# A DMA-bound `x + alpha * fx`: one fifth of x copied from HBM to HBM, and the scaled fx added to it by an accumulating transfer

## The chip, the cores and the metric

The kernel runs on one core of a Trainium2 chip; the other cores are idle. The metric is the device time of one execution in microseconds (us). All times below are medians of executions in the undisturbed ("fast") state, except for the three runs of a single look, whose state is unknown and which are read for their packets and not for a few per cent of time. The span in a profile is about 1.7 us shorter than the time of the same execution.

## The reference

```
B, S, D = 512, 32, 640            # all bfloat16
x, fx: [B, S, D];  alpha: [1]
def reference(x, fx, alpha):
    return x + alpha * fx
```

x, fx and the output have 20.97 MB each. Both inputs must be read once and the output written once: 62.92 MB.

## The kernel before

The tensors are seen as 128 rows (one for each SBUF partition) of 81,920 elements and cut into five chunks of 128 x 16384, which are 4 MiB each. One queue (that of the sync engine, SP) carries every load and store; VectorE computes each chunk with one instruction.

```
xv  = x.flatten_outer_dims().rearrange("(p n) d -> p (n d)", p=P)     # fxv, ov alike
xs = ...tile_pool(name="xs", bufs=4)      # x tiles, 32 KiB a partition
fs = ...tile_pool(name="fs", bufs=2)      # fx tiles
...
def load_x(k):  ... nc.sync.dma_start(out=xt[k][:], in_=xv[:, bass.ts(k, CHUNK)])
def load_f(k):  ... nc.sync.dma_start(out=ft[k][:], in_=fxv[:, bass.ts(k, CHUNK)])
def compute(k, parts=1): ... nc.vector.scalar_tensor_tensor(   # x = f * a + x
        out=xt[k][:, s], in0=ft[k][:, s], scalar=a_f[:], in1=xt[k][:, s],
        op0=ALU.mult, op1=ALU.add)
def store(k, ...): ... nc.sync.dma_start(out=ov[...], in_=xt[k][...])

load_x(0); load_f(0); load_x(1); load_f(1); load_x(2)
compute(0); load_f(2); store(0); load_x(3)
compute(1); load_f(3); store(1); load_x(4)
compute(2); load_f(4); store(2)
compute(3); store(3)
compute(4, 2); store(4, 0, 2); store(4, 1, 2)      # one statement a line in the source
```

Of the kernel before, what the change touches and what calls it, by code (L numbers as in the profile page):

```python
# [1 line left out]

# [4 lines left out]

ACT = mybir.ActivationFunctionType
ALU = mybir.AluOpType
F32 = mybir.dt.float32  # L10
BF16 = mybir.dt.bfloat16

CHUNK = 16384


def alpha_to_lanes(nc, consts, psum, alpha, eng):

    P = nc.NUM_PARTITIONS
    a_1 = consts.tile([1, 1], alpha.dtype, name="a_1")
    eng.dma_start(out=a_1[:], in_=alpha[None, :])  # L20
    ones = consts.tile([1, P], alpha.dtype, name="ones")
    nc.vector.memset(ones[:], 1.0)  # L22
    a_ps = psum.tile([P, 1], F32, name="a_ps")
    nc.tensor.matmul(a_ps[:], ones[:], a_1[:], start=True, stop=True)  # L24
    a_f = consts.tile([P, 1], F32, name="a_f")
    nc.vector.tensor_copy(out=a_f[:], in_=a_ps[:])  # L26
    return a_f


@with_exitstack  # L30
def kernel(
    ctx: ExitStack,
    tc: tile.TileContext,
    x: bass.AP,
    fx: bass.AP,
    alpha: bass.AP,
    out: bass.AP,
):
    nc = tc.nc
    P = nc.NUM_PARTITIONS  # L40
    xv = x.flatten_outer_dims().rearrange("(p n) d -> p (n d)", p=P)
    fxv = fx.flatten_outer_dims().rearrange("(p n) d -> p (n d)", p=P)
    ov = out.flatten_outer_dims().rearrange("(p n) d -> p (n d)", p=P)
    F = xv.shape[1]
    K = F // CHUNK
    assert K * CHUNK == F and K == 5

    consts = ctx.enter_context(tc.tile_pool(name="consts", bufs=1))
    psum = ctx.enter_context(tc.tile_pool(name="psum", bufs=1, space=bass.MemoryType.PSUM))
    xs = ctx.enter_context(tc.tile_pool(name="xs", bufs=4))  # L50
    fs = ctx.enter_context(tc.tile_pool(name="fs", bufs=2))
    ctx.enter_context(tc.manual_schedule())

    a_f = alpha_to_lanes(nc, consts, psum, alpha, nc.scalar)
    xt, ft = {}, {}

    def load_x(k):
        xt[k] = xs.tile([P, CHUNK], x.dtype, tag="x", name="x_t")
        nc.sync.dma_start(out=xt[k][:], in_=xv[:, bass.ts(k, CHUNK)])  # L59

    def load_f(k):
        ft[k] = fs.tile([P, CHUNK], fx.dtype, tag="f", name="f_t")
        nc.sync.dma_start(out=ft[k][:], in_=fxv[:, bass.ts(k, CHUNK)])

    def compute(k, parts=1):
        n = CHUNK // parts
        for j in range(parts):
            s = bass.ts(j, n)
            nc.vector.scalar_tensor_tensor(  # L69
                out=xt[k][:, s],  # L70
                in0=ft[k][:, s],
                scalar=a_f[:],
                in1=xt[k][:, s],
                op0=ALU.mult,
                op1=ALU.add,
            )

    def store(k, j=0, parts=1):
        n = CHUNK // parts
        nc.sync.dma_start(  # L80
            out=ov[:, k * CHUNK + j * n : k * CHUNK + (j + 1) * n],
            in_=xt[k][:, bass.ts(j, n)],
        )

    load_x(0)
    load_f(0)
    load_x(1)
    load_f(1)
    load_x(2)
    compute(0)  # L90
    load_f(2)
    store(0)
    load_x(3)
    compute(1)
    load_f(3)
    store(1)
    load_x(4)
    compute(2)
    load_f(4)
    store(2)  # L100
    compute(3)
    store(3)
    compute(4, 2)
    store(4, 0, 2)
    store(4, 1, 2)


# [1 line left out]
_INS = ['x', 'fx', 'alpha']  # L109
_OUTS = [((512, 32, 640), 'bfloat16')]  # L110


# [23 lines left out]
```

## Time and profile before

| | before |
|---|---|
| time | 152.34 us (152.24 to 152.45, 2 runs) |
| span in the profile | 150.6 us |
| moved by DMA | 62.92 MB, 418 GB/s |
| SP queue's packets, share of the 16 DMA engines' time | 98.0% |
| VectorE busy | 86.9 us (58%) |

These lines are from the page of the kernel before. First come the busy time of the engines, the DMA row of the 40 equal slices of the span (9 means that the 16 DMA engines were busy for 90% or more), then the queues (packets, MB, share of the time of 16 engines), the HBM traffic, the shares of the chain of waits, the costliest group and the DMA issues (out<-in, number, KB each, median us from issue to landing).

```profile
span 150.6 us, 85 instructions
...
PE 0.2 (0%) x1; PEld 0.1 (0%) x1; DVE 86.9 (58%) x8; POOL 0.2 (0%) x4
...
DMA  6999999999999999799999999999999999999994
...
q1 hardware_dynamic: 2304, 62.92, 98.0%
...
HBM read 41.94 MB, written 20.97 MB: 418 GB/s over the span
...
DMA 56%; DVE 29%; DVEq 6%; issue 0%; SPq 0%
...
L69 DVE SCALAR_TENSOR_TENSOR x_t<-f_t,a_f,x_t 128x16384 bf16<-128x16384 bf16 (+1 forms) x6 | 86.6, 14439 | 49.5 <-DMA f_t<-in_fx_dram 49.5
...
f_t<-in_fx_dram SPq DMA_DIRECT2D x5, 4096.0 KB, 32.1
out_dram<-x_t SPq DMA_DIRECT2D x4, 4096.0 KB, 36.5
```

The DMA row is full and the one queue's packets take 98.0% of the engines' time, so the DMA engines are the limit. VectorE waits 49.5 us for fx, which costs nothing by itself: the transfers that it waits for stand in a full queue. And there are 15 transfers of 4 MiB ("units"): 5 + 5 loads and 5 stores (the last one in halves).

The trace also has a record for each packet. Here they are 32,768 B (one row of a chunk), in the kernel before 1.213 us each in the median, for loads and stores alike: 32768 B / 1.213 us = 27.0 GB/s an engine. All data packets together took 147.5 us of all 16 engines (the sum of their durations over 16), so one unit costs 147.5 / 15 = 9.83 us, and the span has 3.1 us more than the packets fill, for the most part at its start and end (the 6 and the 4 of the DMA row).

### The profile page before, as it was taken

The numbers are of one execution on the slowest core, as the hardware profiler recorded it, in microseconds if no ns is written. First come the engines' busy times: TensorE is split into PE (matmuls) and PEld (weight loads), VectorE is DVE, ScalarE is ACT, GpSimd is POOL, SyncE is SP. The second block draws the span as 40 slices with busy tenths as digits, with TensorE's granted clock in tenths as the row PEclk, the third lists the DMA queues.
The fourth block names the chain that finished last, engine by engine and source line by source line (L and its number), as shares of the span: only waits on it lengthen the run. The fifth ranks groups of instructions, "written<-read, shape, count | busy, mean of one in ns | idle before, by whom it ended". The sixth has DMA issues, their size and how long they took to land.

```text
span 150.6 us, 85 instructions
## 1 busy us (share of the span) xinstructions
PE 0.2 (0%) x1; PEld 0.1 (0%) x1; DVE 86.9 (58%) x8; POOL 0.2 (0%) x4
## 2 busy tenths in 40 slices
PE   0000000000000000000000000000000000000000
PEld 0000000000000000000000000000000000000000
DVE  0000009999679998499991006999900089997000
POOL 0000000000000000000000000000000000000000
DMA  6999999999999999799999999999999999999994
GB/s 200 444 453 435 418 418 418 418 444 453 444 453 435 418 418 418 339 444 470 418 418 418 418 418 435 435 435 453 426 435 444 418 418 435 435 435 405 426 444 205
DMA packets 2306, 62.92 MB, mean 418 GB/s; under 512 B 258, under 2 KB 258, under 8 KB 258
## 3 DMA queue, kind: packets, MB, share of 16 engines
q1 hardware_dynamic: 2304, 62.92, 98.0%
q10 hardware_dynamic: 2, 0.00, 0.0%
HBM read 41.94 MB, written 20.97 MB: 418 GB/s over the span
## 4 chain that ended last, share of the span: by engine, by line
DMA 56%; DVE 29%; DVEq 6%; issue 0%; SPq 0%
DMA f_t<-in_fx_dram 56%; DVE x_t L69 29%; DVEq L131 6%; SPq L59 0%; DVEq L69 0%
## 5 line engine op out<-in xcount | busy, mean ns | idle before, releaser
L69 DVE SCALAR_TENSOR_TENSOR x_t<-f_t,a_f,x_t 128x16384 bf16<-128x16384 bf16 (+1 forms) x6 | 86.6, 14439 | 49.5 <-DMA f_t<-in_fx_dram 49.5
L26 DVE COPY a_f<-a_ps 128x1 f32<-128x1 f32 x1 | 0.2, 159 | 1.1 <-PE a_ps L24 1.1
L22 DVE MEMSET ones<- 1x128 bf16 x1 | 0.2, 165 | 0.8 <-PEq L120 0.8
L24 PE MATMUL a_ps<-a,ones 1*128 1x1 bf16 x1 | 0.2, 159 | 1.9 <-DMA a<-in_alpha_dram 1.9
L120 POOL MEMSET const-bfloat16-1.0<- 128x1 bf16 x1 | 0.1, 102 | 0.0
L120 POOL MEMSET const-uint8-127<- 128x1 uint8 x1 | 0.1, 102 | 0.0
L24 PEld LDWEIGHTS <-ones 1*128 1x128 bf16 x1 | 0.1, 100 | 1.0 <-DVE ones L22 1.0
L120 POOL MEMSET const-float32-0.0<- 128x1 f32 x1 | 0.1, 99 | 0.2 <-issue 0.2
L120 POOL MEMSET const-float32-1.0<- 128x1 f32 x1 | 0.1, 99 | 0.0
## 6 DMA issues: line engine op xcount, KB each, us to landing
x_t<-in_x_dram SPq DMA_DIRECT2D x5, 4096.0 KB, 34.8
f_t<-in_fx_dram SPq DMA_DIRECT2D x5, 4096.0 KB, 32.1
out_dram<-x_t SPq DMA_DIRECT2D x4, 4096.0 KB, 36.5
out_dram<-x_t SPq DMA_DIRECT2D x2, 2048.0 KB, 15.2
a<-in_alpha_dram ACTq DMA_DIRECT2D x1, 0.0 KB
```

Of the source, the lines that this page charges most:

```text
L22: nc.vector.memset(ones[:], 1.0)
L24: nc.tensor.matmul(a_ps[:], ones[:], a_1[:], start=True, stop=True)
L26: nc.vector.tensor_copy(out=a_f[:], in_=a_ps[:])
L69: nc.vector.scalar_tensor_tensor(out=xt[k][:, s], in0=ft[k][:, s], scalar=a_f[:], in1=xt[k][:, s], op0=ALU.mult, op1=ALU.add,)
L120: nc = _bacc.Bacc("TRN2", target_bir_lowering=False, num_devices=1)
L131: with _tile.TileContext(nc) as tc:
```

## The change

The intent is to take one x chunk off the way through SBUF and VectorE: chunk 4 of x is copied from HBM straight to the output, and the scaled fx chunk is then added to the output by the DMA engines (`accum_op=ALU.add`). An accumulating transfer has to be issued from GpSimd, by the Trainium skill ("DMA: Bandwidth & Descriptors", SWDGE vs HWDGE vs iDMA). The pieces are cut by `max_dma_last_dim` into 4096 B.

```diff
+    def copy_x(k):
+        return nc.sync.dma_start(out=ov[:, bass.ts(k, CHUNK)], in_=xv[:, bass.ts(k, CHUNK)])
+
+    def scale(k):
+        nc.vector.tensor_scalar_mul(out=ft[k][:], in0=ft[k][:], scalar1=a_f[:])
+
+    def add_store(k):
+        nc.gpsimd.dma_start(
+            out=ov[:, bass.ts(k, CHUNK)],
+            in_=ft[k][:],
+            accum_op=ALU.add,
+            max_dma_last_dim=4096,
+        )
+
     load_x(0)
     load_f(0)
     load_x(1)
     load_f(1)
+    copy_x(4)
     load_x(2)
     compute(0)
     load_f(2)
     store(0)
+    compute(1)
+    load_f(4)
     load_x(3)
-    compute(1)
+    store(1)
+    compute(2)
+    scale(4)
+    add_store(4)
     load_f(3)
-    store(1)
-    load_x(4)
-    compute(2)
-    load_f(4)
     store(2)
-    compute(3)
-    store(3)
-    compute(4, 2)
-    store(4, 0, 2)
-    store(4, 1, 2)
+    compute(3, 2)
+    store(3, 0, 2)
+    store(3, 1, 2)
```

## The prediction

> **What bounds it now.** The page's DMA part gives 62.92 MB in a 150.6 us span, 418 GB/s, with the SP queue's packets filling 98.0% of the time of all 16 DMA engines; the DMA row of the 40 slices reads 9 nearly everywhere. VectorE is busy 58% (86.9 us) and waits 49.5 us for `f_t` loads (groups). The chain of waits alternates `f_t` transfers (56%) and VectorE (29%), but behind it the queue is always full: the engines' time is the limit. There are 15 units of 4 MiB (5 loads of x, 5 of fx, 5 of stores), so one unit costs 150.6 x 0.98 / 15 = 9.84 us (estimate from those figures). Unprofiled time is 1.7 us over the span.
>
> **What the change does.** It removes one x load and one store (2 units, 19.7 us) and one 17.28 us `scalar_tensor_tensor`. It adds an HBM-to-HBM copy (1 unit at a load's rate), an accumulating store, and one `tensor_scalar` on VectorE (a quarter of 17.28 us, 4.4 us, if it does four elements a cycle; not on the limit).
>
> So all hangs on what the accumulating store costs. As a plain store, the sum is 15 units again and nothing is gained. But it must read the SBUF tile and the old output. The Trainium skill ("Collectives: The Full Stack", section on why ReduceScatter is half of AllGather) says that such an add puts two source reads on the same read ring and halves the throughput, measured there as 1.93. So I cost it at 2 units, 19.7 us; no trace here shows it yet. The same section has about 31 GB/s per engine for HBM copies, against 26.6 here (418/16/0.98), so the copy may take 8.5 us (estimate). VectorE's saving is worth nothing.
>
> Sum: 13 plain units 127.9 + copy 8.5 to 9.8 + add 19.7 = 156 to 157.4 us, plus about 3 us idle as now: span near 160.
>
> **Order.** The copy is queued fifth and lands by about 52 us, so the add never waits for it. Fx chunk 4 should land near 91, its scaling near 96, so the accumulating transfer starts near 97, while x3, store 1, fx 3 and store 2 are queued. It shares the engines with fx 3, the last input, which lands near 121 unshared, 127 to 140 shared, followed by two 8.7 us computes and a half store (5 to 7 us). With even sharing this tail ends near 163; if the SP queue's large packets win, the add finishes last, near 160. GpSimd must also write descriptors, some us, mostly hidden.
>
> **Predicted:** 162 us, 155 to 174 eight times in ten. Faster by over 2%: 0.06; within 2%: 0.13; slower: 0.81.
>
> **What would show it.** A second, software queue of 4.19 MB whose packets take about 12% of the engines' span (6% would mean one unit); SP queue 58.7 MB and about 85%; HBM read 46.1 MB if the old output's read is counted; the copy 8 to 10 us of engine time; VectorE busy near 74 us; DMA slices 9 until the tail; fx 3 landing after 121 us, and the chain ending in fx 3's transfer, VectorE, then the last half store (or the accumulating transfer).
>
> **What would make it wrong.** The old output's reads overlapping the SBUF reads (add of 1 unit: 150 to 153 us); the copy far below the load rate (170 us and more) or far above it, if the SBUF side is what limits 26.6 GB/s (148 us); an add limited by its small descriptors or by GpSimd's writing of them (over 170 us).

## The result

The changed kernel takes 165.84 us (165.21 to 166.46, 2 runs) against 152.34 us. The ratio is 1.0877, with a 95% interval of 1.0801 to 1.0953. (Ratios and intervals are from fast runs; they are not quite the ratios of the medians quoted, which here would be 1.0886.)

These are the same lines of the page of the changed kernel, with the new queue and the new issues.

```profile
span 164.7 us, 83 instructions
...
PE 0.2 (0%) x1; PEld 0.1 (0%) x1; DVE 74.1 (45%) x8; POOL 1.9 (1%) x5
...
DMA  7999999999999899999999999999999999999992
...
q1 hardware_dynamic: 2160, 58.72, 85.4%
q0 software_dynamic: 1040, 4.19, 12.8%
...
HBM read 41.94 MB, written 25.17 MB: 407 GB/s over the span
...
DMA 57%; DVE 26%; DVEq 5%; SPq 0%; issue 0%
...
L69 DVE SCALAR_TENSOR_TENSOR x_t<-f_t,a_f,x_t 128x16384 bf16<-128x16384 bf16 (+1 forms) x5 | 69.3, 13870 | 68.6 <-DMA f_t<-in_fx_dram 68.6
L89 DVE TENSOR_SCALAR f_t<-f_t,a_f 128x16384 bf16<-128x16384 bf16 x1 | 4.5, 4485 | 2.1 <-DMA f_t<-in_fx_dram 2.1
...
f_t<-in_fx_dram SPq DMA_DIRECT2D x5, 4096.0 KB, 34.7
...
out_dram<-in_x_dram SPq DMA_DIRECT2D x1, 4096.0 KB, 51.1
out_dram<-f_t POOLq DMA_DIRECT2D x1, 4096.0 KB, 64.5
out_dram<-x_t SPq DMA_DIRECT2D x2, 2048.0 KB, 12.5
```

The two queues together carried the same 62.92 MB as the one queue before, and the DMA row is still full up to its last slice. VectorE lost 12.8 us of work, to no effect. The copy, issued at 2.7 us, landed 51.1 us later, long before the add went out. What grew is the time that the same bytes take on the DMA engines. The new software queue (GpSimd's, q0) has 4.19 MB, 6.7% of the bytes, but takes 12.8% of the engines. The SP queue still takes 85.4% of a longer span (140.6 us) although 4.19 MB less pass through it. "HBM written" grew from 20.97 to 25.17 MB, because chunk 4 of the output is written twice, by the copy and by the add. "HBM read" didn't grow with the add: if the old output is read, this count leaves it out.

The packet records of the two traces give the account (my sums of packet durations over 16 engines, in us):

```
                              before     after
SP queue, all data packets     147.5     140.5
GpSimd queue, the add              -      21.0
sum                            147.5     161.5
span                           150.6     164.7
idle (span - sum)                3.1       3.2

packet, median us
32768 B load or store           1.213    1.213 (1.226 beside the add)
32768 B copy HBM to HBM             -    1.48
4096 B adding packet                -    0.327
```

The growth of the sum, 14.0 us, is the growth of the span, 14.1 us. So there is no new idle time to explain, only dearer packets: the add costs 21.0 us where a plain unit costs 9.83, which is 11.2 us of the growth. Of the rest, about 2 us are the copy's own, which at 1.48 us a packet should cost about 12 us; the last 0.8 us or so lie with loads and stores beside the two.

The end of the span shows in the chain of waits of the changed kernel (start us, us, what) and in the waits of the SP queue (engine and line, what it waited for, total us, times, longest us).

```profile
40.22 34.70 DMA f_t<-in_fx_dram
...
75.02 17.30 DVE x_t L69
...
92.33 36.92 DMA f_t<-in_fx_dram
...
129.35 8.75 DVE x_t L69
138.10 8.66 DVEq L145
```

```profile
SPq L145 <- DMA out_dram<-f_t: 16.4, 1, 16.4
```

Fx chunk 3, the last input, lands at 129.3 us; the two half computes end at 146.8. Line 145 is the end of the program: what it waited for last, 16.4 us long, is the landing of the add. The add was issued at 99.2 us and took 64.5 us to land for only 21.0 us of work, because it shared the engines with the SP queue. In the 34 us after its first packet, while the SP queue was full, 379 packets of 4096 B and 345 packets of 32,768 B were started: about one for one, whatever their size, so that the add got only about a quarter of the engines (379 x 0.327 / 16 = 7.7 of 34 us).

### The profile page after: what moved, and what is told of

Same layout as the page of the kernel before. It is cut to its first block, busy times and chain, and to the rows that moved or that the text cites. A ratio compares the mean times of both kernels' runs of the same rounds, so it can differ in the third digit from the quotient of the medians.

```text
span 164.7 us, 83 instructions
## 1 busy us (share of the span) xinstructions
PE 0.2 (0%) x1; PEld 0.1 (0%) x1; DVE 74.1 (45%) x8; POOL 1.9 (1%) x5
## 2 busy tenths in 40 slices
DMA packets 3202, 62.92 MB, mean 382 GB/s; under 512 B 258, under 2 KB 258, under 8 KB 1282
## 3 DMA queue, kind: packets, MB, share of 16 engines
q1 hardware_dynamic: 2160, 58.72, 85.4%
q0 software_dynamic: 1040, 4.19, 12.8%
HBM read 41.94 MB, written 25.17 MB: 407 GB/s over the span
## 4 chain that ended last, share of the span: by engine, by line
DMA 57%; DVE 26%; DVEq 5%; SPq 0%; issue 0%
DMA f_t<-in_fx_dram 57%; DVE x_t L69 26%; DVEq L145 5%; SPq L59 0%; DVEq L69 0%
## 5 line engine op out<-in xcount | busy, mean ns | idle before, releaser
L69 DVE SCALAR_TENSOR_TENSOR x_t<-f_t,a_f,x_t 128x16384 bf16<-128x16384 bf16 (+1 forms) x5 | 69.3, 13870 | 68.6 <-DMA f_t<-in_fx_dram 68.6
L89 DVE TENSOR_SCALAR f_t<-f_t,a_f 128x16384 bf16<-128x16384 bf16 x1 | 4.5, 4485 | 2.1 <-DMA f_t<-in_fx_dram 2.1
L92 POOL DMA_DIRECT2D out_dram<-f_t x1 | 1.7, 1678 | 98.8 <-DVE f_t L89 98.8
## 6 DMA issues: line engine op xcount, KB each, us to landing
out_dram<-in_x_dram SPq DMA_DIRECT2D x1, 4096.0 KB, 51.1
out_dram<-f_t POOLq DMA_DIRECT2D x1, 4096.0 KB, 64.5
out_dram<-x_t SPq DMA_DIRECT2D x2, 2048.0 KB, 12.5
```

The source lines that it names most:

```text
L69: nc.vector.scalar_tensor_tensor(out=xt[k][:, s], in0=ft[k][:, s], scalar=a_f[:], in1=xt[k][:, s], op0=ALU.mult, op1=ALU.add,)
L89: nc.vector.tensor_scalar_mul(out=ft[k][:], in0=ft[k][:], scalar1=a_f[:])
L92: nc.gpsimd.dma_start(out=ov[:, bass.ts(k, CHUNK)], in_=ft[k][:], accum_op=ALU.add, max_dma_last_dim=4096,)
```

## The experiments

The theory after reading the traces has two parts. **T1:** an adding packet reads two sources, the SBUF tile and the old output, one after the other, so it takes twice the time of a plain one. **H1:** a copy that runs on all 16 engines at once is slowed by the HBM itself, because it both reads and writes there; at 1.48 us a packet, 32768 B x 16 / 1.48 us = 354 GB/s are read and 354 GB/s written, 708 GB/s in sum. The Trainium skill ("HBM Reference", Specifications (TRN2)) has about 716 GB/s for an HBM domain. The rivals are given with each experiment. Edits are against the changed kernel, but for those of `copy_half` and `early_add2`, which are shown against `contig` and `early_add`. `plain_add`, `no_copy`, `copy_act` and `early_add` share runs of the kernel before (152.56 us without the two slow ones of its seven executions), `add_2k`, `add_fp32`, `contig` and `early_add2` share others (152.91 us), and `copy_half` had one of its own (152.47 us, state unknown).

### 1. The addition taken out (`plain_add`)

```diff
-            accum_op=ALU.add,
```

> The same kernel with the addition taken out of the GpSimd transfer, still 1024 descriptors of 4096 B from GpSimd; wrong result on purpose. Theory T1 (the add costs a second read): the software queue's share falls from 12.8% to about 6.5% (about 10 us of all engines), and the kernel takes about 155 us. Rival T2 (small descriptors or GpSimd's writing of them cost the time): share stays near 12.8% and the time near 166 us.

Measured: 156.43 us, ratio to the kernel before 1.0224 (1.0146 to 1.0302); the result is wrong. These are the lines of its queues on its page.

```profile
span 153.8 us, 83 instructions
...
q1 hardware_dynamic: 2160, 58.72, 91.0%
q0 software_dynamic: 1040, 4.19, 6.6%
```

The packets fell from 0.327 to 0.159 us and their sum from 21.0 to 10.2 us (6.6% of 153.8). The same 1024 packets from the same GpSimd queue without the addition are nearly as cheap as large ones (a perfect eighth of 1.213 us would be 0.152). So neither the small descriptors nor GpSimd's writing of them are the cost; the addition is, with 10.8 us. T2 falls.

### 2. The copy left out (`no_copy`)

```diff
-    copy_x(4)
```

> The changed kernel without the HBM-to-HBM copy, so the add falls on whatever the output held; wrong result on purpose. The copy's packets in the trace took 1.48 us in the median against 1.21 us for a load's. If those sums are right the copy costs about 12 us of all engines and the kernel takes about 153.5 us; if a copy costs the same as a load (9.8 us), about 156 us.

Measured: 153.77 us, 12.1 us under the changed kernel's 165.84 (these two come from different rounds; the kernel before differed by 0.2 us between them). The result is wrong. The SP queue's sum of packets fell from 140.5 to 128.7 us, by 11.8. The copy costs about 12 us, not 9.8. Even without any copy the kernel only draws level with the kernel before (ratio 1.0073, 0.9981 to 1.0166).

### 3. The copy on another queue (`copy_act`)

```diff
-        return nc.sync.dma_start(out=ov[:, bass.ts(k, CHUNK)], ...
+        return nc.scalar.dma_start(out=ov[:, bass.ts(k, CHUNK)], ...
```

> The copy issued from ScalarE's queue, so that its packets alternate with the first loads instead of running alone; result right. Theory H1 (a copy running alone asks the HBM for 16 engines' read plus write, some 700 GB/s, and the HBM is the limit): interleaved, its packets take about 1.21 us, its own queue's share is about 6.0%, the kernel gains about 2.3 us, near 163.5 us. Rival H2 (an HBM-to-HBM packet takes an engine longer by itself): packets stay at 1.48 us, share about 7.2%, time unchanged near 166 us.

Measured: correct, 163.64 us, ratio to the kernel before 1.0688 (1.0594 to 1.0783). The lines of its queues on its page (q10 is now the copy's):

```profile
span 161.8 us, 83 instructions
...
q1 hardware_dynamic: 2016, 54.53, 79.4%
q0 software_dynamic: 1040, 4.19, 13.0%
q10 hardware_dynamic: 146, 4.19, 6.1%
```

6.1% of 161.8 us are 9.9 us: issued beside the first loads, the copy's packets took 1.213 us in the median, exactly a load's, and the kernel gained 2.2 us (between different rounds; the sum of all packets fell by 2.5 us, from 161.5 to 159.0). A packet from HBM to HBM is therefore not slow by itself; H2 falls in that form. What remains open here is whether it is the HBM, or copies that follow each other on one engine (H2b), or the layout of the rows (H3).

### 4. Rows without a pitch (`contig`)

Chunks were taken as contiguous blocks in all transfers; the result stays the same.

```diff
-    xv = x.flatten_outer_dims().rearrange("(p n) d -> p (n d)", p=P)        # fxv, ov alike
+    xv = x.flatten_outer_dims().rearrange("r d -> (r d)").rearrange("(k p n) -> k p n", k=5, p=P)
-    ... xv[:, bass.ts(k, CHUNK)] ...
+    ... xv[k] ...
```

> Every chunk taken as one contiguous 4 MiB block (row pitch 32 KiB instead of 160 KiB) in all transfers, copy still alone in the SP queue; result right. H1 (the copy's read and write together reach what the HBM gives): its packets stay near 1.48 us and the time near 166 us. Rival H3 (the pitch of the rows makes source and destination collide in the HBM): packets fall to 1.21 us, time near 163.5 us.

Measured: correct, 165.90 us, ratio 1.0852 (1.0776 to 1.0927); no gain. The copy, now one run of bytes, was cut into 64 packets of 65,536 B instead of 128 of 32,768 B; they took 2.88 us in the median, which is 22.7 GB/s an engine, hardly more than the 22.1 GB/s of before. Twice the packet size and another pitch leave the rate where it was. H3 falls.

### 5. The copy on half of the engines (`copy_half`)

In the contiguous layout, the copy is named as 8 rows, 0.8% short, so that only 8 engines take part (the edit is shown against `contig`; that the copy's 64 packets of 2.4 us were all started within 17.4 us fits 8 engines):

```diff
-        return nc.sync.dma_start(out=ov[k], in_=xv[k])
+        flat = lambda v: v[k].rearrange("p n -> (p n)").rearrange("(a b) -> a b", a=8)[:, :260096]
+        return nc.sync.dma_start(out=flat(ov), in_=flat(xv))
```

> The copy put on 8 of the 16 engines (8 rows of 520192 B, 0.8% short so that they stay apart; wrong result on purpose), back to back as before, while the other 8 engines go on with loads. In the contiguous layout its 65536 B packets took 2.88 us on all 16 engines (22.7 GB/s an engine). H1 (the sum of the copy's reads and writes reaches what the HBM gives): at half the engines 65024 B packets take about 2.41 us (27.0 GB/s). Rival H2b (copies following each other on one engine are slow, whatever the other engines do): about 2.87 us. The kernel gets slower than 166 us either way, as the engines are loaded unevenly by some 10 us.

Measured (one look, state unknown): 172.77 us; the result is wrong, as intended. Packet records, size and median us:

```
copy_half   65024 B on 8 engines    2.399    27.1 GB/s an engine
contig      65536 B on 16 engines   2.883    22.7 GB/s an engine
```

Still one after the other in the same queue, the copies run at the full rate of an engine when only half of the engines copy and the other half load. H2b falls. The three runs leave H1: 16 engines copying ask for 16 x 27.0 x 2 = 864 GB/s of reads and writes and got about 710; half of them copying and half loading ask for 8 x 54 + 8 x 27 = 648 GB/s and got it. That the ceiling sits in the HBM, and not in something on the way to it that copies also share, is argued from the agreement with the skill's figure (708 and 726 GB/s, against about 716) and not shown; the runs show only that 16 engines copying at once are held below their full rate, and that 8 copying beside 8 loading are not.

### 6. The adding packets cut in two (`add_2k`)

```diff
-            max_dma_last_dim=4096,
+            max_dma_last_dim=2048,
```

> The adding transfer cut into 2048 descriptors of 2048 B instead of 1024 of 4096 B; result right. The add's packets took 0.327 us against 0.159 us for the same packets without the addition. T1 (a second read of the same bytes at the same rate): a 2048 B packet takes about 0.16 to 0.18 us, the software queue's sum stays at 21 to 23 us, time near 166 to 168 us. Rival T4 (a fixed delay of about 0.17 us for every adding descriptor, such as waiting for the old bytes): about 0.25 us a packet, sum about 32 us, time near 176 us.

Measured (one look, state unknown): correct, 166.8 us; 0.178 us a packet, sum 22.8 us. The line of the queue on its page:

```profile
q0 software_dynamic: 2064, 4.19, 13.8%
```

Half the bytes take 0.178 / 0.327 = 54% of the time. The two sizes give a fixed part of 2 x 0.178 - 0.327 = 0.029 us a packet (an estimate that assumes a straight line), and a part that grows with the bytes, 0.298 us for 4096 B, which is 27.5 GB/s if 8192 B are counted. A delay of 0.17 us for each adding descriptor (T4) would have given 0.25 us; T4 falls.

### 7. The same bytes added as float32 (`add_fp32`)

```diff
-            out=ov[:, bass.ts(k, CHUNK)],
-            in_=ft[k][:],
+            out=ov[:, bass.ts(k, CHUNK)].bitcast(F32),
+            in_=ft[k][:].bitcast(F32),
```

> The same bytes added as float32 (half the elements in each 4096 B packet); wrong result on purpose. T1 (bytes read decide): packets stay at 0.327 us, software queue near 21 us, time near 166 us. Rival T3 (the adder's element rate decides): packets fall to between 0.16 and 0.25 us, the queue's sum to 10 to 16 us and the time to 155 to 161 us.

Measured (one look, state unknown): 167.1 us, wrong as intended; the packets took 0.327 us, unchanged, with half as many elements. The element rate of the adder (T3) isn't the limit. Of the theories named T1 is left: what the addition costs grows with the bytes and equals a second passage of the same bytes (0.327 against 2 x 0.159 us). That this passage is the read of the old output is argued from what an add needs and from the section of the Trainium skill that the prediction cites; no record of the trace shows that read by itself. An adder that is itself limited in bytes, and not in elements, to about this rate would look the same in these runs; that rival stands untested.

### 8. The add issued early (`early_add`, `early_add2`)

The first try moves the copy up behind the first two loads and loads the add's fx chunk directly after it, with 3 buffers for x and 3 for fx (the order is shown in short; lines only taken away from their old places are left out):

```diff
-    xs = ...tile_pool(name="xs", bufs=4)
-    fs = ...tile_pool(name="fs", bufs=2)
+    xs = ...tile_pool(name="xs", bufs=3)
+    fs = ...tile_pool(name="fs", bufs=3)
+    (tiles of fx chunks 0, 1 and 4 taken from fs ahead of the loads)
     load_x(0); load_f(0)
+    copy_x(4); load_f(4)
     load_x(1); load_f(1); load_x(2)
     compute(0)
+    scale(4); add_store(4)
     load_f(2); store(0); compute(1)
+    load_f(3); store(1); load_x(3)
     compute(2); store(2)
     ...
```

> The add issued near 48 us instead of 99 us (its fx chunk loaded second, 3 buffers each for x and fx); result right. Theory W (the engines' total work is the limit, so the place of the add is worth nothing): 163 to 166 us. Rival L (the add is late, and as the last to land it makes the end): near 155 us.

Measured: correct, 173.70 us, ratio 1.1363 (1.1285 to 1.1440). This was a miss of the design: the waits of the SP queue show a load of fx (line 64) that stood until the add had landed, so its buffer came free only then.

```profile
SPq L64 <- DMA out_dram<-f_t: 72.9, 1, 72.9
```

So it says nothing on W against L, only that a buffer read by an accumulating transfer can be held long (63.9 us from issue to landing here). The second try gives the tile of fx chunk 4 a pool of its own (shown against the first try; x keeps its 3 buffers, one fewer than in the changed kernel):

```diff
+    f4 = ...tile_pool(name="f4", bufs=1)
-    fs = ... bufs=3
+    fs = ... bufs=2
-        ft[k] = fs.tile(...)
+        ft[k] = (f4 if k == 4 else fs).tile(...)
```

> The early add again, with the tile for its fx chunk in a pool of its own, so that no later load waits for the add to land (in the first try the SP queue stood 72.9 us on that wait). Theory W (total engine work is the limit): 163 to 166 us, with the DMA row full. Rival L (the add being last to land makes the end): near 155 us.

Measured: correct, 168.46 us, ratio 1.1022 (1.0975 to 1.1069). This is slower than both expectations. The DMA row and the issue of the add on its page:

```profile
span 166.8 us, 85 instructions
...
DMA  7899999999999999999999999999999999997555
...
out_dram<-f_t POOLq DMA_DIRECT2D x1, 4096.0 KB, 96.0
```

The sum of all packets is 160.9 us, as in the changed kernel (161.5), so the work was not reduced by its place: L falls, and the 166.8 us of span are that sum and 5.9 us of idle time, 2.7 more than in the changed kernel. Most of the idle time is in the last four slices (7555): the add, issued at 49.6 us, had landed by 146, and nothing was left to fill the engines while VectorE computed the last halves. In the changed kernel the late add fills this gap. My number for W (163 to 166 us) left that out. The place of the add is not the only difference, though: the load of the last x chunk (line 60) stood 19.4 us until a store had landed and its buffer, one of only 3, came free. It was issued at 104.4 us, against 60.0 in the changed kernel, and landed at 142.1, so that the last halves started late. How much of the 2.7 us is due to that buffer was not tested.

```profile
SPq L60 <- DMA out_dram<-x_t: 19.4, 1, 19.4
```

No experiment points to a version that beats the kernel before. The best of the change is `copy_act` (163.64 us). Even an add that cost no more than a plain store would leave the 15 units of before.

## Why the prediction was right, and where its steps were not

- **The bound** was right: the sum of packets grew by 14.0 us and the span by 14.1.
- **VectorE's saving is worth nothing** was right: busy 74.1 us (predicted 74), `tensor_scalar` 4.485 us (predicted 4.4).
- **"I cost it at 2 units, 19.7 us"** was right as far as the runs go. Experiments 1, 6 and 7 show that the addition is the cost, that it goes with the bytes and that neither elements nor descriptors decide it. That the cost is a second read is argued (experiment 7). The term was 1.3 us too small (21.0 us); the fixed part of 1024 small packets, 0.029 x 1024 / 16 = 1.9 us (an estimate), is large enough for that. The section of the Trainium skill cited in the prediction ("Collectives: The Full Stack", The bandwidth ceiling) agrees: 1.93 there, for ring collectives, and 0.327 / 0.159 = 2.06 here.
- **"The copy may take 8.5 us (estimate)"** is the step that failed. It measured about 12 us. The rate of 31 GB/s an engine that I took from the same section was for a step of a ring collective, with two engines at work; I carried it to sixteen and didn't ask what they ask of the HBM together. Experiments 3, 4 and 5 show an engine's copy at 27.0 GB/s when not all 16 copy, and at 22 GB/s when they do. What could have warned me, the figure for an HBM domain, stood in the skill's "HBM Reference".
- **The sum** was therefore 156 to 157.4 us instead of 161.5: 2.2 to 3.5 us from the copy, 1.3 us from the add, and some 0.6 us from packets beside them. Both errors go the same way, so that the time fell within the range because the range was wide enough for them, not because they cancelled. Span 160 was predicted and 164.7 measured; the time of 165.84 lies in the range, 2.4% above the centre of 162.
- **The order** was right: scaling ended at 98.9 us (predicted 96), the add went out at 99.2 (97), fx 3 landed at 129.3 (127 to 140). Of the two tails the second came true: the SP queue's large packets won and the add landed last. The half stores took 12.5 us to land, not 5 to 7, as they too shared the engines with the add.
- **The marks**: SP queue 85.4% (about 85%), software queue 12.8% (about 12%); HBM read stayed at 41.94 MB, so the page doesn't count a read of the old output.

## What to carry to other kernels

Where the DMA engines are the limit, count engine time and not bytes through SBUF: an accumulating store took a plain store's time twice, so that it gave back the load that it was meant to save, and a compute instruction saved beside a full DMA row was worth nothing. Copies from HBM to HBM should be mixed with other transfers (a second queue was enough), since 16 engines that all copy ran at 22 GB/s each and not at 27. A transfer cut into small packets lands late beside a queue of large ones: plan for a buffer that it holds long, and for whether it fills the tail or leaves it empty.

## What the Trainium skill lacked or had wrong

- "DMA: Bandwidth & Descriptors" has no rate an engine for a copy from HBM to HBM, and nothing on how many engines copy at once; its only rates for such copies stand in the row on HBM row pitch, under other conditions. Here it was 27.0 GB/s an engine mixed with loads, and 22.1 to 22.7 GB/s with all 16 engines copying, 708 to 726 GB/s of reads and writes in sum; "HBM Reference" has the 716 GB/s that this agrees with, but doesn't say that a copy would count twice.
- "DMA: Bandwidth & Descriptors" has no cost for an accumulating transfer from SBUF: 0.327 us for 4096 B against 0.159 us for the same packet without the addition, 0.178 us for 2048 B. The factor stands only under collectives.
- The same page (Queues, rings and completion order) gives some 9 to 17 descriptors as typical of what an engine takes from one queue before it changes to another. The records here show 379 of 4096 B and 345 of 32,768 B in the same 34 us, about one for one. Joined end to start into 16 chains (the records don't name the engine), they change queue at about three of four steps in the first 24 us of the add, and at about nine of ten in `early_add2`, with no run of nine.
